# Two persistent two-bank PSUM tiles become a pool of tiles: two-bank for the first batch, then four single-bank tiles in rotation

## The chip, the cores and the metric

The kernel runs on one core of one Trainium2 chip. The metric is the device time of one execution in microseconds; the runs of a kernel are given by their median. The times of the stages come from one profiled execution.

The core's engines work from queues of their own, each in the order of the program, and wait for each other through semaphores: PE multiplies matrices into PSUM, ACT and DVE read PSUM and work element by element, POOL works on SBUF only, SP issues most of the DMAs (ACT and POOL issue some too). PSUM has 8 banks of 512 fp32 columns by 128 partitions; the kernel uses all of them.

## The reference

Attention at two scales for 8 batches of 8 heads, 576 positions of 64 values, followed by a two-layer network over all 4608 tokens:

```python
q_d = q.reshape(B, H, Sd, 4, D).mean(axis=3)      # k_d, v_d alike: Sd = 144 coarse positions
out_up = np.repeat(sm_attn(q_d, k_d, v_d), 4, axis=2)
mask = np.abs(pos[:, None] - pos[None, :]) < 4    # local attention
out_local = softmax(where(mask, scale * q @ k.T, -1e9)) @ v
x = (out_up + out_local).transpose(0, 2, 1, 3).reshape(4608, 512)
h = x @ w_in                                      # 512 -> 2048
g = np.where(h > 0.0, h, np.exp(np.minimum(h, 0.0)) - 1.0)
out = g @ w_out                                   # 2048 -> 512
```

## The kernel before

**Attention.** A batch is done in four pairs of heads. `pair_transposes` (L568) turns q and k of a pair around on PE into the PSUM tiles tq and tk, adds the coarse sums of v on PE into the free columns of tq, and has ACT copy them to qt and kt and DVE copy vd; POOL forms the coarse sums of q and k from the copies. `pair_scores` (L579) multiplies local and coarse scores into two PSUM tiles sc; ACT takes exp of each in two parts (pex, dex, L278 and L283), DVE masks (mex, L293). `denominators` (L307) sums the exps of all four pairs on PE into one bank den, and DVE takes the reciprocal rc (L333). `spread_out` and `spread_in` (L337, L341) send rc to DRAM and read it back spread over partitions (rd, rcb); ACT's queue issues these DMAs. `pair_outputs` (L602) multiplies exps and v for two pairs into two tiles lg, DVE multiplies by rcb (gn, ln, L427 and L430), and POOL adds both into xt (L438), the transposed input of the network. `first_batch` (L509) does batch 0 in a form of its own, on the two duo tiles and the tiles tagged "two".

**The network.** Tokens go in 9 blocks t of 512. `mm1(t, fc)` (L448) forms 128 of the 2048 hidden values of a block with four matmuls into one bank hp (L454). ACT reads the bank for e = exp (L459), DVE takes min and subtracts 1 (L460), and DVE reads the bank again for gt = max(hp, 0) + e (L463), which is the bank's last reader. `mm2(t, i)` (L467) does a quarter of the 16 matmuls of 128 tokens into a bank op (L474); with the last quarter ACT copies op to os (L480) and SP writes it out.

**PSUM.** Four of the 8 banks are two buffers of two banks each, tagged "two" (L96), which tq, tk, sc, lg and others take in turn. The other four are the tiles duo[0] and duo[1] (L99), two banks each, which live through the whole kernel. After the first batch, `bank(i)` (L297) gives bank i of these four: mm1 takes banks 0 and 1 (duo[0]) in turn, except in block 0, which takes 0, 2, 1, 3; `misc_bank` (L300) gives 2 and 3 (duo[1]) in turn to den and op.

**The order of the work** is written out by hand as a list of events with times (L609 to L645), sorted once. The unit is a slot: `mm1(t, s)` stands at 16t + s + 0.25 and `mm2(t, s)` at 16(t + 1) + s + 0.75, so that each slot from 16 to 143 holds one mm1 of block t and one mm2 of the block before; the last 16 slots hold mm2 alone. Batch b >= 3 starts at base = 16b - 25: its transposes stand at base + 0, 1.6, 4.8 and 9.7, its scores at base + 3.2, 6.4, 11.3 and 12.9, denominators at 14.5, `spread_out` and `spread_in` at 16.1 and 17.1, its outputs at 21 and 22.6, in the middle of the next batch. Batch 1 stands beside block 0, batch 2 from slot 12 on in a denser order. The last outputs are at slot 109.6, so slots 111 to 143 hold the network alone.

Of the kernel before, what the change touches and what calls it, by code (L numbers as in the profile page):

```python
# [10 lines left out]
FP32 = mybir.dt.float32  # L11
AB = mybir.AluOpType
AF = mybir.ActivationFunctionType
# [59 lines left out]
def kernel(  # L73
# [9 lines left out]
    nc = tc.nc  # L83
    sb = ctx.enter_context(tc.tile_pool(name="sb", bufs=1))
    ps = ctx.enter_context(tc.tile_pool(name="ps", bufs=1, space=bass.MemoryType.PSUM))
# [10 lines left out]
    def two(name):  # L96
        return ps.tile([128, 1024], FP32, tag="two", bufs=2, name=name)

    duo = [ps.tile([128, 1024], FP32, tag=f"duo{i}", bufs=1, name=f"duo{i}") for i in range(2)]  # L99

    def g2(ap, a, n):

# [2 lines left out]
    def h2(ap):  # L105
        return ap.rearrange("p (g u) -> p g u", g=2)
# [3 lines left out]
    WI = sb.tile([128, DMC, DFF], FP16, tag="WI", bufs=1, name="WI")  # L110
    WO = sb.tile([128, FCN, DM], FP16, tag="WO", bufs=1, name="WO")
# [134 lines left out]
    def scores(b, j, e, sc, masked):  # L246
        s = st[(b, j)]
        r = slice(64 * e, 64 * e + 64)
        if masked:
            for g in range(2):  # L250
                nc.tensor.matmul(
                    sc[0:KW, 512 * g : 512 * g + HB], C["NI"][:, 0:KW],
                    C["NI"][:, KW + HB * g : KW + HB * g + HB], start=True, stop=False,
                )
        for c in range(NB):
            a = 512 * (c // 3) + QB * (c % 3)
            nc.tensor.matmul(
                sc[0:KW, a : a + QB], s["kt"][r, QB * c : QB * c + KW],
                s["qt"][r, QB * c : QB * c + QB], start=not masked,
                stop=not masked or c % 3 == 2,  # L260
            )

    def coarse(b, j, e, sc):
        s = st[(b, j)]
        r = slice(64 * e, 64 * e + 64)
        for kg in range(2):
            nc.tensor.matmul(
                sc[0:KG, 512 * kg + HB : 512 * kg + HB + SD],
                s["kd"][r, KG * kg : KG * kg + KG], s["qd"][r, :], start=True, stop=True,
            )  # L270

    def exp_local(b, j, e, sc):
        s = st[(b, j)]
        if e == 0:
            s["pex"] = sb.tile([KW, 2, S], FP16, tag="mex" if b == 0 else "pex",
                               bufs=8 if b == 0 else 2, name="pex")
            s["dex"] = sb.tile([KG, 2, 2, SD], FP16, tag="dex", bufs=8, name="dex")
        nc.scalar.activation(  # L278
            out=h2(s["pex"][:, e, :]), in_=g2(sc[0:KW], 0, HB), func=AF.Exp, scale=SCALE
        )  # L280

    def exp_coarse(b, j, e, sc):
        nc.scalar.activation(  # L283
            out=st[(b, j)]["dex"][:, e], in_=g2(sc[0:KG], HB, SD), func=AF.Exp,
            scale=SCALE / 16,
        )
# [5 lines left out]
        mk2 = bass.AP(tensor=mk.tensor, offset=mk.offset, ap=[list(mk.ap[0]), [0, 2], [1, S]])  # L292
        nc.vector.tensor_tensor(out=s["mex"][:], in0=s["pex"][:], in1=mk2, op=AB.mult)  # L293

    misc = [0]

    def bank(i, n=512):  # L297
        return duo[i // 2][:, 512 * (i % 2) : 512 * (i % 2) + n]

    def misc_bank():  # L300
        misc[0] += 1
        return bank(2 + misc[0] % 2)


    RC = {}

    def denominators(b):  # L307
        den = misc_bank()
        for j in range(NPAIR):
            nc.tensor.matmul(  # L310
                den[32 * j : 32 * j + 32, 0:HB], C["SEED"][:, 32:64], C["SEED"][:, 64 + SD :],
                start=True, stop=False, tile_position=(0, 32 * j),
            )
        for e in range(2):
            for g in range(2):
                r = 2 * e + g
                for j in range(NPAIR):
                    nc.tensor.matmul(
                        den[32 * j : 32 * j + 32, 0:HB], C["IND"][0:KW, 31 - r : 63 - r],
                        st[(b, j)]["mex"][:, e, HB * g : HB * g + HB],  # L320
                        start=False, stop=False, tile_position=(0, 32 * j),
                    )
        for e in range(2):
            for kg in range(2):
                r = 4 + e
                for j in range(NPAIR):
                    nc.tensor.matmul(
                        den[32 * j : 32 * j + 32, 0:SD], C["IND"][0:KG, 31 - r : 63 - r],
                        st[(b, j)]["dex"][:, e, kg, :], start=False,
                        stop=(e == 1 and kg == 1), tile_position=(0, 32 * j),  # L330
                    )
        rc = RC[b] = sb.tile([128, HB], FP16, tag="rc", bufs=1, name="rc")
        nc.vector.reciprocal(out=rc[:], in_=den[:, 0:HB])  # L333
# [112 lines left out]
    gts, ops = {}, {}  # L446

    def mm1(t, fc):  # L448
        if fc == 0:
            gts[t] = sb.tile([128, FCN, TBLK], FP16, tag="gt", bufs=2, name="gt")  # L450
        hp = bank((0, 2, 1, 3)[fc % 4]) if t == 0 else bank(fc % 2)
        x = xts[t]
        for dc in range(DMC):
            nc.tensor.matmul(  # L454
                hp, WI[:, dc, 128 * fc : 128 * fc + 128], x[:, dc, :],
                start=(dc == 0), stop=(dc == DMC - 1),
            )
        e = sb.tile([128, TBLK], FP16, tag="e", bufs=3, name="e")
        nc.scalar.activation(out=e[:], in_=hp, func=AF.Exp)  # L459
        nc.vector.tensor_scalar(  # L460
            out=e[:], in0=e[:], scalar1=1.0, scalar2=-1.0, op0=AB.min, op1=AB.add
        )
        nc.vector.scalar_tensor_tensor(  # L463
            out=gts[t][:, fc, :], in0=hp, scalar=0.0, op0=AB.max, in1=e[:], op1=AB.add
        )

    def mm2(t, i):  # L467

        tt, part = i // 4, i % 4
        if part == 0:  # L470
            ops[t] = misc_bank()
        op_ = ops[t]
        for fc in range(4 * part, 4 * part + 4):
            nc.tensor.matmul(  # L474
                op_, gts[t][:, fc, 128 * tt : 128 * tt + 128], WO[:, fc, :],
                start=(fc == 0), stop=(fc == FCN - 1),
            )
        if part == 3:
            os_ = sb.tile([128, DM], FP32, tag="os", bufs=3, name="os")
            nc.scalar.copy(out=os_[:], in_=op_)  # L480
            r = TBLK * t + 128 * tt
            nc.sync.dma_start(out=out[r : r + 128, :], in_=os_[:])

# [25 lines left out]
    def first_batch():  # L509
        b = 0  # L510
        transposes(b, 0)
        evict_q(b, 0, act)
        evict_k(b, 0, act)
        sums(b, 0, "q")
        sums(b, 0, "k")
        load_qk(1, 0)
        for j in range(NPAIR):
            for e in range(2):
                scores(b, j, e, duo[e], True)
            if j < 3:  # L520
                transposes(b, j + 1)
            exp_local(b, j, 0, duo[0])
            exp_local(b, j, 1, duo[1])
            for e in range(2):
                coarse(b, j, e, duo[e])
            if j < 3:
                evict_q(b, j + 1, act)
            exp_coarse(b, j, 0, duo[0])
            if j < 3:
                evict_k(b, j + 1, act)  # L530
                sums(b, j + 1, "q")
                sums(b, j + 1, "k")
                load_qk(1, j + 1)
            exp_coarse(b, j, 1, duo[1])
            st[(b, j)]["mex"] = st[(b, j)]["pex"]
        for j in range(NPAIR):
            load_v(1, j)
        for h in range(2):
            dv = two("dv") if h == 0 else duo[0]
            den_half(b, h, dv)  # L540
            for i in range(2):
                v_sums(b, 2 * h + i, dv[0:KG, 512 + 256 * i : 768 + 256 * i], 128)
            vd = sb.tile([KG, 512], FP16, tag="vd2", bufs=2, name="vd2")
            dve(out=vd[:], in_=dv[0:KG, 512:1024])
            rbs = {}
            for i in range(2):
                j = 2 * h + i
                st[(b, j)]["vd"] = vd[:, 256 * i : 256 * i + 256]
                rbs[j] = two("rb")
                spread_pe(b, j, rbs[j])  # L550
            for i in range(2):
                j = 2 * h + i
                copy = act if h == 1 else dve
                spread_copy(b, j, rbs[j], copy, copy)
            for i in range(2):
                j = 2 * h + i
                lg = two("lg") if h == 0 else duo[i]
                outputs(b, j, lg)
                normalise(b, j, lg)
        for n in range(8):  # L560
            load_wo(n)
# [46 lines left out]

    at(-10, first)  # L609
    at(-9, first_batch)  # L610

    def loads(b, j):
# [62 lines left out]
```

## Time and profile before

| What | Value |
|---|---|
| median of 3 runs | 542.28 us (539.0 to 543.46) |
| profiled execution, its own time | 540.33 us |
| its span, first to last instruction | 538.5 us |
| mean granted TensorE clock | 0.971 |
| PE busy | 391.8 us (73%) |
| DVE busy | 233.5 us (43%) |
| ACT busy | 201.9 us (37%) |
| POOL busy | 143.3 us (27%) |
| mm1 matmuls (L454): busy, idle before them | 155.5 us, 92.3 us |
| mm2 matmuls (L474): busy, idle before them | 150.4 us, 16.5 us |

The first mm1 starts at 41.5 us, the first mm2 at 95.7, the mm1 of slot 39 at 178.7, that of slot 103 at 403.3, that of slot 111 at 427.1, and the mm2 of the last block alone begin at 518.3.

How to read the profile: a line of the waits names the engine and line that stood idle, what it waited for, the total in us, the number of times and the longest. A line of the timeline has start and duration in us, engine, line, operation, tile written <- tiles read, shape, xcount, and in brackets the idle time ahead of it and what ended it. PE's duration of a group runs to the end of its last matmul, so groups that follow without a gap overlap a little in the rows. A line of the windows has the stretch, its length, the busy time of PE, PEld (weight load), DVE, ACT and POOL with counts, the granted clock, the share of the DMA engines and GB/s.

### The profile page before, as it was taken

What the parts mean: (1) busy time and instruction counts of PE and PEld (TensorE: products, weight loads), DVE (VectorE), ACT (ScalarE), POOL (GpSimd) and SP (SyncE); (2) the same over time, 40 slices, a digit from 0 to 9 for tenths busy, and PEclk for the clock granted to TensorE, in tenths of its full rate; (3) what the DMA queues carried; (4) which work ended last, traced back from release to release, by engine and by line L of the source; (5) the groups of instructions that cost most, each with busy time, mean ns of one, the idle gap of its engine ahead of it and who ended that gap; (6) DMA issues with size and microseconds to landing.
All of it is one profiled execution on the core that took longest, in us unless ns stands there. A gap on an engine that the chain in (4) does not pass through costs nothing.

```text
span 538.5 us, 8199 instructions
## 1 busy us (share of the span) xinstructions
PE 391.8 (73%) x3164; PEld 208.0 (39%) x3164; DVE 233.5 (43%) x431; ACT 201.9 (37%) x377; POOL 143.3 (27%) x241
## 2 busy tenths in 40 slices
PE   4875966877886867776686778776766766676676
PEld 3663543443443444344344434343332322222232
DVE  2252765335455355524544464446443633333320
ACT  4601753453334344524362535253432222222211
POOL 4418444342340333213421252035200300000000
PEclk9999996899799999989999999899999999999999
DMA  9999998375540771348143934020002000000011
GB/s 188 209 195 172 201 177 158 71 154 129 116 90 21 164 145 48 63 114 161 39 107 75 176 60 110 7 74 21 21 25 75 27 34 19 19 21 39 19 40 58
DMA packets 130884, 49.02 MB, mean 91 GB/s; under 512 B 115324, under 2 KB 126238, under 8 KB 130846
## 3 DMA queue, kind: packets, MB, share of 16 engines
q1 hardware_dynamic: 115018, 36.97, 32.8%
q0 software_dynamic: 6480, 5.38, 6.3%
q10 hardware_dynamic: 9348, 6.16, 5.2%
q8 instruction: 25, 0.41, 0.3%
q14 instruction: 13, 0.11, 0.1%
HBM read 43.91 MB, written 9.95 MB: 100 GB/s over the span
## 4 chain that ended last, share of the span: by engine, by line
PE 45%; DVE 24%; ACT 17%; issue 5%; ACTq 3%; POOL 3%; DMA 3%; DVEq 0%; POOLq 0%
PE duo L454 21%; DVE gt L463 11%; PE duo L474 11%; ACT e L459 9%; DVE e L460 6%; ACTq L346 3%; ACT pex L278 3%; DVE rc L333 3%; PE tk L199 2%; ACT dex L283 2%; PE tq L199 2%; PE lg L411 2%; DMA rd<-rc 2%; DVE mex L293 2%; PE tq L240 1%
## 5 line engine op out<-in xcount | busy, mean ns | idle before, releaser
L454 PE MATMUL duo<-xt,WI 128*128 128x512 f16 x576 | 155.5, 392 | 92.3 <-DVE gt L463 86.6
L459 ACT ACTIVATE e<-duo 128x512 f16<-128x512 f32 x144 | 86.0, 599 | 241.9 <-PE duo L454 232.2
L474 PE MATMUL duo<-WO,gt 128*128 128x512 f16 x576 | 150.4, 388 | 16.5 <-DVE rc L333 13.7
L460 DVE TENSOR_SCALAR e<-e 128x512 f16<-128x512 f16 x144 | 48.0, 333 | 191.7 <-ACT e L459 191.1
L454 PEld LDWEIGHTS <-WI 128*128 128x128 f16 x576 | 54.9, 99 | 172.6 <-issue 115.9
L463 DVE SCALAR_TENSOR_TENSOR gt<-duo,e 128x512 f16<-128x512 f32 x144 | 99.6, 692 | 5.4
L474 PEld LDWEIGHTS <-gt 128*128 128x128 f16 x576 | 55.5, 99 | 84.4 <-issue 23.9
L232 POOL TENSOR_TENSOR t<-qt 128x288 f32<-128x288 f16 x28 | 18.6, 664 | 189.0 <-ACT qt L212 189.0
L438 POOL TENSOR_TENSOR xt<-ln,gn 128x512 f16<-128x512 f16 (+7 forms) x64 | 41.9, 685 | 82.8 <-DVE ln L430 82.8
L278 ACT ACTIVATE pex<-sc 112x576 f16<-112x576 f32 x56 | 36.2, 647 | 8.4 <-PE sc L593 7.6
L212 ACT CAST qt<-tq 128x576 f16<-128x576 f32 x32 | 20.4, 638 | 36.7 <-PE tq L240 32.6
L293 DVE TENSOR_TENSOR mex<-pex,MASK 112x1152 f16<-112x1152 f16 x28 | 21.9, 782 | 25.1 <-ACT pex L278 25.1
L480 ACT COPY os<-duo 128x512 f32<-128x512 f32 x36 | 21.1, 586 | 22.6 <-PE duo L474 22.6
L181 POOL CAST v<-v 112x768 f16<-112x768 f32 x32 | 27.2, 864 | 6.9 <-DMA v<-in_v_dram 6.7
L575 DVE CAST vd<-tq 72x256 f16<-72x256 f32 x28 | 11.7, 419 | 30.9 <-ACT qt L212 30.9
L411 PE MATMUL lg<-mex,v 112*64 112x96 f16 x336 | 14.1, 228 | 12.8 <-ACT dex L283 6.8
L283 ACT ACTIVATE dex<-sc 72x288 f16<-72x288 f32 x56 | 22.6, 404 | 0.0
L430 DVE TENSOR_TENSOR ln<-lg,rcb 128x576 f16<-128x576 f32 x30 | 22.4, 748 | 0.0
L199 PEld LDWEIGHTS tq<-I,q 96*128 96x128 f32 x168 | 18.4, 149 | 8.5 <-issue 2.8
L411 PEld LDWEIGHTS <-v 112*64 112x64 f16 x384 | 14.4, 129 | 17.9 <-issue 14.1
L218 ACT CAST kt<-tk 128x576 f16<-128x576 f32 x32 | 20.6, 644 | 0.1
L199 PE MATMUL tq<-I,q 96*128 96x96 f32 x168 | 19.7, 256 | 1.1 <-ACT dex L283 1.1
(74 smaller groups left out, 293.2 us busy)
## 6 DMA issues: line engine op xcount, KB each, us to landing
v<-in_v_dram SPq DMA_DIRECT2D x30, 336.0 KB, 4.9
out_dram<-os SPq DMA_DIRECT2D x36, 256.0 KB, 2.0
q<-in_q_dram SPq DMA_DIRECT2D x56, 144.0 KB, 3.3
k<-in_k_dram SPq DMA_DIRECT2D x56, 144.0 KB, 3.9
rcb<-rd ACTq DMA_DIRECT2D x14, 288.0 KB, 5.0
WO<-in_moe_w_out_dram POOLq DMA_DIRECT2D x8, 256.0 KB, 8.9
WI<-in_moe_w_in_dram POOLq DMA_DIRECT2D x3, 512.0 KB, 11.6
rcb<-rd ACTq DMA_DIRECT2D x14, 72.0 KB, 5.0
```

What stands on the lines that cost most here:

```text
L181: nc.gpsimd.tensor_copy(out=v16[:], in_=v32[:].rearrange("p (e c) d -> p c e d", e=2))
L199: nc.tensor.transpose(t[:, a : a + QB], x[:, c, :, :].rearrange("p e d -> p (e d)"), C["I32"][:])
L278: nc.scalar.activation(out=h2(s["pex"][:, e, :]), in_=g2(sc[0:KW], 0, HB), func=AF.Exp, scale=SCALE)
L283: nc.scalar.activation(out=st[(b, j)]["dex"][:, e], in_=g2(sc[0:KG], HB, SD), func=AF.Exp, scale=SCALE / 16,)
L293: nc.vector.tensor_tensor(out=s["mex"][:], in0=s["pex"][:], in1=mk2, op=AB.mult)
L411: nc.tensor.matmul(lg[64 * e : 64 * e + 64, a : a + QB], v16[:, c, e, :], s["mex"][:, e, QB * c : QB * c + QB], start=True, stop=True,)
L438: nc.gpsimd.tensor_tensor(out=xt(t)[:, j, t0 - TBLK * t : t1 - TBLK * t], in0=ln[:, a:z], in1=_rep4(gn[:, a // 4 : z // 4]), op=AB.add,)
L454: nc.tensor.matmul(hp, WI[:, dc, 128 * fc : 128 * fc + 128], x[:, dc, :], start=(dc == 0), stop=(dc == DMC - 1),)
L459: nc.scalar.activation(out=e[:], in_=hp, func=AF.Exp)
L460: nc.vector.tensor_scalar(out=e[:], in0=e[:], scalar1=1.0, scalar2=-1.0, op0=AB.min, op1=AB.add)
L463: nc.vector.scalar_tensor_tensor(out=gts[t][:, fc, :], in0=hp, scalar=0.0, op0=AB.max, in1=e[:], op1=AB.add)
L474: nc.tensor.matmul(op_, gts[t][:, fc, 128 * tt : 128 * tt + 128], WO[:, fc, :], start=(fc == 0), stop=(fc == FCN - 1),)
```

## The change

The two tiles duo[0] and duo[1] are no longer made once. For the first batch they come from a pool `fp` of their own, a new tile for every use (`duo(i, name)`). At the first call of `bank` that pool is closed and a pool `late` opened on the four banks, with two tags of two single-bank buffers each: "hp" for mm1, "misc" for den, op, and the odd fc of block 0. Every den, op and hp is now a tile of its own. Which buffer comes next is still taken in turn, and the events and the operations are the same.

```diff
-    duo = [ps.tile([128, 1024], FP32, tag=f"duo{i}", bufs=1, name=f"duo{i}") for i in range(2)]
+    front = ctx.enter_context(ExitStack())
+    fp = front.enter_context(tc.tile_pool(name="fp", bufs=1, space=bass.MemoryType.PSUM))
+    late = {}
+
+    def duo(i, name):
+        return fp.tile([128, 1024], FP32, tag=f"duo{i}", bufs=1, name=name)
...
-    misc = [0]
-
-    def bank(i, n=512):
-        return duo[i // 2][:, 512 * (i % 2) : 512 * (i % 2) + n]
-
-    def misc_bank():
-        misc[0] += 1
-        return bank(2 + misc[0] % 2)
-
+    def bank(tag, name):
+        if not late:
+            front.close()
+            late["ps"] = ctx.enter_context(
+                tc.tile_pool(name="late", bufs=1, space=bass.MemoryType.PSUM)
+            )
+        return late["ps"].tile([128, 512], FP32, tag=tag, bufs=2, name=name)
...
-        den = misc_bank()
+        den = bank("misc", "den")
...
-        hp = bank((0, 2, 1, 3)[fc % 4]) if t == 0 else bank(fc % 2)
+        hp = bank("misc" if t == 0 and fc % 2 else "hp", "hp")
...
-            ops[t] = misc_bank()
+            ops[t] = bank("misc", "op")
...
         for j in range(NPAIR):
+            sc = [duo(e, "sc") for e in range(2)]
             for e in range(2):
-                scores(b, j, e, duo[e], True)
+                scores(b, j, e, sc[e], True)
...
-            dv = two("dv") if h == 0 else duo[0]
+            dv = two("dv") if h == 0 else duo(0, "dv")
...
-                lg = two("lg") if h == 0 else duo[i]
+                lg = two("lg") if h == 0 else duo(i, "lg")
```

In first_batch the operands `duo[0]` and `duo[1]` of the exps and coarse scores become `sc[0]` and `sc[1]`; in mm1 and mm2 `hp` and `op_` become `hp[:]` and `op_[:]`.

More of the change, by code (lines that the diff above doesn't have):

```diff
@@ L454, in mm1 @@
             nc.tensor.matmul(
-                hp, WI[:, dc, 128 * fc : 128 * fc + 128], x[:, dc, :],
+                hp[:], WI[:, dc, 128 * fc : 128 * fc + 128], x[:, dc, :],
                 start=(dc == 0), stop=(dc == DMC - 1),
@@ L458, in mm1 @@
         e = sb.tile([128, TBLK], FP16, tag="e", bufs=3, name="e")
-        nc.scalar.activation(out=e[:], in_=hp, func=AF.Exp)
+        nc.scalar.activation(out=e[:], in_=hp[:], func=AF.Exp)
         nc.vector.tensor_scalar(
@@ L463, in mm1 @@
         nc.vector.scalar_tensor_tensor(
-            out=gts[t][:, fc, :], in0=hp, scalar=0.0, op0=AB.max, in1=e[:], op1=AB.add
+            out=gts[t][:, fc, :], in0=hp[:], scalar=0.0, op0=AB.max, in1=e[:], op1=AB.add
         )
@@ L474, in mm2 @@
             nc.tensor.matmul(
-                op_, gts[t][:, fc, 128 * tt : 128 * tt + 128], WO[:, fc, :],
+                op_[:], gts[t][:, fc, 128 * tt : 128 * tt + 128], WO[:, fc, :],
                 start=(fc == 0), stop=(fc == FCN - 1),
@@ L479, in mm2 @@
             os_ = sb.tile([128, DM], FP32, tag="os", bufs=3, name="os")
-            nc.scalar.copy(out=os_[:], in_=op_)
+            nc.scalar.copy(out=os_[:], in_=op_[:])
             r = TBLK * t + 128 * tt
@@ L517, in first_batch @@
         for j in range(NPAIR):
+            sc = [duo(e, "sc") for e in range(2)]
             for e in range(2):
-                scores(b, j, e, duo[e], True)
+                scores(b, j, e, sc[e], True)
             if j < 3:
                 transposes(b, j + 1)
-            exp_local(b, j, 0, duo[0])
-            exp_local(b, j, 1, duo[1])
+            exp_local(b, j, 0, sc[0])
+            exp_local(b, j, 1, sc[1])
             for e in range(2):
-                coarse(b, j, e, duo[e])
+                coarse(b, j, e, sc[e])
             if j < 3:
                 evict_q(b, j + 1, act)
-            exp_coarse(b, j, 0, duo[0])
+            exp_coarse(b, j, 0, sc[0])
             if j < 3:
@@ L533, in first_batch @@
                 load_qk(1, j + 1)
-            exp_coarse(b, j, 1, duo[1])
+            exp_coarse(b, j, 1, sc[1])
             st[(b, j)]["mex"] = st[(b, j)]["pex"]
```

## The prediction

> **What bounds the kernel now.** I read the share of busy time first (PE 73%, DVE 43%, ACT 37%: no engine is full), then the list of waits, and there who holds up PE, since PE has the most work.
>
> ```profile
> PE duo L454 <- DVE gt L463: 86.6, 96, 1.8
> PE duo L474 <- DVE rc L333: 13.7, 6, 2.5
> PE lg L411 <- ACT dex L283: 6.8, 9, 1.4
> PE lg L411 <- DVE vd L575: 4.9, 4, 1.2
> PE duo L474 <- ACT os L480: 2.9, 4, 0.7
> ```
>
> PE stands for 86.6 us in 96 waits ahead of mm1 (L454) until VectorE has written gt (L463), which is the last reader of an mm1 bank. Which group's gt? The timeline of the late stage, where only mm1 and mm2 are left, shows it:
>
> ```profile
> 454.83 1.02 PE L454 MATMUL duo<-xt,WI 128*128 128x512 f16 x4 [0.88 <-DVE gt L463]
> 455.69 1.03 PE L474 MATMUL duo<-WO,gt 128*128 128x512 f16 x4
> 455.90 0.60 ACT L459 ACTIVATE e<-duo 128x512 f16<-128x512 f32 x1 [2.17 <-PE duo L454]
> 456.53 0.29 DVE L460 TENSOR_SCALAR e<-e 128x512 f16<-128x512 f16 x1 [1.74 <-ACT e L459]
> 456.86 0.69 DVE L463 SCALAR_TENSOR_TENSOR gt<-duo,e 128x512 f16<-128x512 f32 x1
> 457.60 1.02 PE L454 MATMUL duo<-xt,WI 128*128 128x512 f16 x4 [0.88 <-DVE gt L463]
> ```
>
> The mm1 at 457.60 starts 0.05 after the gt that belongs to the mm1 of 454.83, its direct predecessor, although the two write different banks (fc % 2). So the two halves of one duo tile are held apart as if they were one buffer, and each slot is a serial chain matmul, exp, min, add, matmul of 2.77 us. PE's own part is 454.83 to 455.69 (0.86) and about as much for mm2. The same holds for duo1: mm2 waits for the reciprocal (rc) and for os, which read its other bank.
>
> Then the stages, by windows (us, PE, PEld, DVE, ACT, POOL, clock, DMA share, GB/s): slots 16 to 38, four periods of 16 slots with one batch of attention each, slots 103 to 110, and the 33 slots without attention.
>
> ```profile
> 96.00:178.60 82.60, 64.91 (x553) 35.36 (x552) 38.51 (x69) 35.38 (x68) 23.56 (x39) 0.92 0.43 95
> 178.60:236.00 57.40, 42.43 (x370) 22.66 (x368) 26.56 (x49) 23.28 (x44) 17.01 (x28) 0.97 0.48 99
> 291.60:348.40 56.80, 42.28 (x367) 22.66 (x365) 26.36 (x49) 23.28 (x44) 17.23 (x29) 0.97 0.48 100
> 403.30:427.10 23.80, 16.85 (x128) 7.64 (x128) 12.14 (x24) 5.95 (x10) 4.86 (x8) 1.00 0.19 54
> 427.10:518.20 91.10, 62.30 (x264) 25.51 (x264) 32.33 (x66) 24.92 (x42) 0.41 (x1) 1.00 0.06 24
> ```
>
> In a period of 57 us DVE works 26.5, ACT 23.3, POOL 17 and DMA 27 (0.48): a PE that goes faster has room on all of them down to about 40 us.
>
> **The change part by part.** *What it does not touch.* In the two compiled programs every engine has the same instructions in the same order (PE 5994, DVE 433, ACT 421, POOL 246, SP 184); no DMA is added or moved past another. Only PSUM addresses and waits differ. In the list of waits, an mm1 of t > 0 now waits for the gt two groups back, where it waited for one back; op and den wait for the reader two allocations back. So five prices, by stage.
>
> *1. The 33 last slots.* An mm1's gt is done 2.77 after its start (454.83 to 457.60). With two free banks the wait decides only if two slots are shorter than that. A slot of PE alone is 0.86 + 0.87 (326.76 to 327.62, 325.89 to 326.76) = 1.735, two are 3.47: no wait. DVE needs 0.33 + 0.69 and ACT 0.6 + 0.59/4 of it. 33 x 1.735 = 57.3 in place of 91.2: saves 33.9.
>
> *2. The last token block.* Its 64 mm2 run as 4 x 16 with 0.72 between for os; 16 take 3.61 with 0.16 of fill, 3.45 back to back. The stretch from 518.29 to 534.92 becomes 13.96: saves 2.7.
>
> *3. A period of 16 slots.* PE issue, from rows where the next one follows at once: 32 groups at 0.87 (27.8), 4 pairs' transposes at 1.33 (295.55 to 296.88), 4 scores at 0.57 (330.54 to 331.11), 2 output pairs at 0.89 (309.20 to 310.09), denominators 1.09 (125.55 to 126.64): 38.3. What stays: the tiles tagged "two" are not changed, and their waits remain.
>
> ```profile
> 309.20 0.45 PE L411 MATMUL lg<-mex,v 112*64 112x96 f16 x12 [1.24 <-DVE vd L575]
> 315.94 0.45 PE L411 MATMUL lg<-mex,v 112*64 112x96 f16 x12 [1.09 <-ACT dex L283]
> 316.78 0.45 PE L411 MATMUL lg<-mex,v 112*64 112x96 f16 x12 [0.26 <-ACT dex L283]
> 294.41 2.63 ACTq L346 DMA_DIRECT2D rcb<-rd  x4
> ```
>
> Outputs right behind transposes cost 1.24 to 1.4, right behind scores 1.35; both are set by ACT and DVE, not by duo. The third is new. ACT's queue issues four rcb transfers (2.63 us) once rd has landed, 2.4 after its issue (291.98 to 294.41). Today PE waits meanwhile anyway. Scheduled by hand from the period's first transposes: rd at 2.2, rcb issues 4.6 to 7.3, exp of the second slot to 7.9, second pair's kt copied by 9.1; PE reaches the scores that need this buffer at 7.9, so it waits 1.3. Sum 38.3 + 4.0 = 42.3. I carried the hand schedule through all 16 slots with the durations above: the nearest an mm1 comes to its gt is 0.76 (the slot behind the first scores, whose exps hold ACT for 1.77). The mm2 that waited 1.1 to 2.5 for rc goes straight on, since rc reads the other bank; DVE is held for the same 1.95, and the mm1 that needs the gt behind it stands two slots and a set of transposes later. Today's four periods last from 177.3 to 403.3, 226; 4 x 42.3 = 169: saves 57. Bounds: 38.3 with none of the stalls (16 more saved), and 47 if every one of the 8 transposes and scores adds 0.6 (19 less). I take 42.3, nearer to what the L411 rows show.
>
> *4. Slots 16 to 38* (95.7 to 177.3, 81.6). 23 x 1.74 + 6 transposes + 7 scores + 2 output pairs + 2 denominators = 40.0 + 8.0 + 4.0 + 1.8 + 2.2 = 56; the same kinds of stall (1.24, 1.35, 1.3 and some 0.9 for the xt of slot 32) 4.8; the slow start (mm2 at 95.70 takes 1.71, transposes 1.70) 1.2. 62: saves 20, bounds 12 and 24. *Slots 103 to 110*: 8 x 1.74 + 1.8 + 1.8 behind the last rcb issues = 17.5 in place of 23.8: saves 6.3.
>
> *5. Before 95.7: nothing.* In the first batch each tile is still taken when its forerunner's readers are done, as now. The pool's end makes the first mm1 wait for both last ln; its fourth matmul waits for xt (43.83) as before, so at most 0.7 and likely 0. The 2.82 that mm1 waits for rc at 76.3 goes, but the cover moves: ACT issues rcb from 81.13 to 83.75, so the transposes' copies and the scores at 84.99 come no sooner, and PE waits 5.4 there in place of 2.62. From 85 on outputs, ln and xt form the chain. 0, bounds 0 and 2.8.
>
> Sum: 33.9 + 2.7 + 57 + 20 + 6.3 = 119.9. The profiled span 538.5 becomes 418.6, and with the 1.83 around it (540.33 less 538.5) 420.4. The median of the runs (542.28) is 1.95 above that execution: 422.
>
> **A rule that speaks against it.** The granted clock is below 1 only around long gaps: 0.66 in 80 to 100, where PE stood 2.6 and 2.8 us; in the last stage, with a 0.88 gap in each slot, it is 1.00. The Trainium skill, "TensorE: Matmul & The Clock Gate", section "A second HAM failure mode: psum-queue depth-cycling", says that cycling through PSUM banks with N = 512 lets PE idle often enough for its clock to go up and down. Here, by the rows, gaps of 0.88 did not do that, so the trace does not bear it out; it is the third rival all the same.
>
> **The rivals.** *The waits come back elsewhere.* In-order ACT and DVE queues could keep mm1 waiting in slots 16 to 110, where exps (1.77), mask (0.76) and normalising (1.85) stand ahead of its own. Today 57.8 of the 86.6 lie there. If half survive, 29 and 5 of fills are lost: 456. For it: ACT e waits and DVE e waits are the largest rows after all. Against: ACT and DVE busy 23 and 26 in 42.
>
> *The change does nothing*: a new tile waits for all of the pool's readers, so the chain stands, 542. Against: the lists of waits name the gt two back.
>
> *The clock falls, and it gets slower.* PE issue from 95.7 on is 56 + 153 + 15.7 + 57 + 14 = 296 at full clock. If the denser bank cycling held the clock at c, 296 x (1/c - 1) is added; it eats the 119.9 at c = 0.71. At the 0.66 of 80 to 100 it is 152: 574. Only in the last 33 slots: 57.3 x 0.52 = 30, 452. Against: the matmul rows of 16 in a row (518.29, 3.61) ran at full clock.
>
> **How the numbers follow.** Forecast 0.82; waits elsewhere 0.11; clock in the last slots only 0.02; clock throughout 0.03; nothing 0.02. Faster by over 1% (about what a measurement of this kernel can tell from no change): 0.82 + 0.11 + 0.02 = 0.95; within 1% 0.02; slower 0.03. Range: down to 411 with about half of the period bound's 16 and a little of stage 4's, up to 442 with the 19 of the upper one; this leaves out the rivals.
>
> **What would show it.** The row "PE duo L454 <- DVE gt L463" nearly gone, late slots 1.74 apart, periods near 42, "PE L474 <- DVE rc" and "<- ACT os" gone, L411 waits as today or larger, PE about 92% of the span after 96, clock 1.00. Wrong: mm1 waits of a microsecond behind scores; slots of 2 us or more in the last stage; matmul rows above 0.4 us.

## The result, and the profile after

| | Before | After |
|---|---|---|
| median | 542.87 us (4 runs, 539.0 to 543.65) | 422.81 us (4 runs, 421.59 to 424.91) |
| profiled execution, span | 540.33 us, 538.5 us | 424.91 us, 423.1 us |
| PE busy, share of the span | 391.8 us, 73% | 371.9 us, 88% |

The ratio is 0.780 (95% interval 0.775 to 0.785). The forecast was 422 (411 to 442). Line numbers of the changed kernel are 3 to 5 higher: mm1 L457, exp L462, gt L466, mm2 L477, os L483, rcb L349.

First the waits of PE in the changed kernel. The row "PE duo L454 <- DVE gt L463" (86.6 us in 96 waits) has become the last of these, 1.9 us in 2 waits, and rows of mm2 on rc or os no longer exist. What stands on top now are users of the two-bank tiles tagged "two" (sc, lg), on ACT and DVE.

```profile
PE sc L590 <- DVE vd L579: 7.8, 4, 6.1
PE lg L414 <- ACT dex L288: 6.7, 10, 1.1
PE lg L414 <- DVE vd L579: 4.9, 4, 1.2
PE hp L457 <- DVE gt L466: 1.9, 2, 1.0
```

The timeline of the last stage shows how the chain came apart (start and duration first, in us):

```profile
348.56 1.03 PE L457 MATMUL hp<-xt,WI 128*128 128x512 f16 x4
349.42 1.03 PE L477 MATMUL op<-WO,gt 128*128 128x512 f16 x4
349.62 0.60 ACT L462 ACTIVATE e<-hp 128x512 f16<-128x512 f32 x1 [1.13 <-PE hp L457]
350.25 0.36 DVE L463 TENSOR_SCALAR e<-e 128x512 f16<-128x512 f16 x1 [0.24 <-ACT e L462]
350.28 1.03 PE L457 MATMUL hp<-xt,WI 128*128 128x512 f16 x4
350.64 0.69 DVE L466 SCALAR_TENSOR_TENSOR gt<-hp,e 128x512 f16<-128x512 f32 x1
```

The mm1 at 350.28 starts while the chain of its forerunner (348.56) has only come to the min; that forerunner's gt ends at 351.33. PE has no idle time in brackets, and a slot lasts 1.73 in place of 2.77, though exp and gt take as long as before (0.60 and 0.69). By windows (PE, PEld, DVE, ACT, POOL, clock, DMA share, GB/s) for the four periods, slots 103 to 110 and the 33 last slots:

```profile
159.60:204.00 44.40, 40.99 (x369) 22.73 (x367) 26.67 (x49) 23.18 (x44) 16.90 (x28) 0.96 0.62 127
204.00:248.40 44.40, 40.91 (x367) 22.62 (x365) 26.67 (x49) 23.18 (x44) 16.90 (x28) 0.96 0.65 128
248.40:291.10 42.70, 39.20 (x367) 22.20 (x365) 26.31 (x49) 23.18 (x44) 17.32 (x29) 1.00 0.68 133
291.10:331.50 40.40, 37.82 (x351) 20.68 (x349) 26.01 (x47) 23.17 (x44) 15.44 (x26) 1.00 0.15 47
331.50:348.50 17.00, 15.98 (x130) 7.66 (x128) 11.62 (x25) 5.85 (x11) 3.33 (x6) 1.00 0.31 80
348.50:405.50 57.00, 57.00 (x266) 25.83 (x264) 33.07 (x67) 24.38 (x41) 1.95 (x3) 1.00 0.10 38
```

ACT and DVE do the same work per period as before (23 and 26 to 27 us), in 43 us in place of 56; in the last line PE is busy all of the time. The first two lines have a granted clock of 0.96; that was not forecast, and is taken up below.

### The profile page after: what moved, and what is told of

The parts are those of the page before. It is cut to its first block, busy times and chain, and to the rows that moved or that the text cites. A ratio compares the mean times of both kernels' runs of the same rounds, so it can differ in the third digit from the quotient of the medians.

```text
span 423.1 us, 8180 instructions
## 1 busy us (share of the span) xinstructions
PE 371.9 (88%) x3164; PEld 205.9 (49%) x3164; DVE 234.0 (55%) x431; ACT 200.8 (47%) x377; POOL 143.1 (34%) x241
## 4 chain that ended last, share of the span: by engine, by line
PE 74%; ACT 6%; DVE 5%; POOL 4%; DMA 4%; ACTq 3%; issue 3%; DVEq 0%; POOLq 0%
PE op L477 28%; PE hp L457 26%; ACTq L349 3%; PE tk L204 3%; PE tq L204 3%; PE sc L590 2%; DMA rd<-rc 2%; POOL xt L441 2%; PE lg L414 2%; PE tq L245 2%; ACT e L462 2%; ACT dex L288 2%; ACT pex L283 1%; PE sc L262 1%; POOL WO L125 1%
## 5 line engine op out<-in xcount | busy, mean ns | idle before, releaser
L457 PE MATMUL hp<-xt,WI 128*128 128x512 f16 x576 | 154.2, 391 | 5.9 <-POOL xt L441 2.5
L462 ACT ACTIVATE e<-hp 128x512 f16<-128x512 f32 x144 | 86.0, 600 | 136.0 <-PE hp L457 114.8
L477 PE MATMUL op<-WO,gt 128*128 128x512 f16 x576 | 148.1, 385 | 0.0
L466 DVE SCALAR_TENSOR_TENSOR gt<-hp,e 128x512 f16<-128x512 f32 x144 | 99.6, 692 | 5.4
L463 DVE TENSOR_SCALAR e<-e 128x512 f16<-128x512 f16 x144 | 49.8, 346 | 86.3 <-ACT e L462 84.3
L457 PEld LDWEIGHTS <-WI 128*128 128x128 f16 x576 | 54.8, 100 | 70.4 <-issue 11.4
L477 PEld LDWEIGHTS <-gt 128*128 128x128 f16 x576 | 55.0, 99 | 66.0 <-issue 4.3
L283 ACT ACTIVATE pex<-sc 112x576 f16<-112x576 f32 x64 | 41.4, 648 | 11.7 <-PE sc L262 5.8
L483 ACT COPY os<-op 128x512 f32<-128x512 f32 x36 | 21.1, 586 | 18.8 <-PE op L477 18.8
L288 ACT ACTIVATE dex<-sc 72x288 f16<-72x288 f32 x64 | 25.9, 405 | 0.9 <-PE sc L272 0.9
L590 PE MATMUL sc<-qt,kt 64*112 64x96 f16 x336 | 15.5, 219 | 11.4 <-DVE vd L579 7.8
L414 PE MATMUL lg<-mex,v 112*64 112x96 f16 x336 | 12.2, 210 | 13.5 <-ACT dex L288 6.7
L590 PEld LDWEIGHTS <-kt 64*112 64x112 f16 x336 | 12.5, 129 | 22.9 <-issue 21.0
```

What stands on the lines that cost most here:

```text
L283: nc.scalar.activation(out=h2(s["pex"][:, e, :]), in_=g2(sc[0:KW], 0, HB), func=AF.Exp, scale=SCALE)
L288: nc.scalar.activation(out=st[(b, j)]["dex"][:, e], in_=g2(sc[0:KG], HB, SD), func=AF.Exp, scale=SCALE / 16,)
L414: nc.tensor.matmul(lg[64 * e : 64 * e + 64, a : a + QB], v16[:, c, e, :], s["mex"][:, e, QB * c : QB * c + QB], start=True, stop=True,)
L457: nc.tensor.matmul(hp[:], WI[:, dc, 128 * fc : 128 * fc + 128], x[:, dc, :], start=(dc == 0), stop=(dc == DMC - 1),)
L462: nc.scalar.activation(out=e[:], in_=hp[:], func=AF.Exp)
L463: nc.vector.tensor_scalar(out=e[:], in0=e[:], scalar1=1.0, scalar2=-1.0, op0=AB.min, op1=AB.add)
```

## The experiments

Two theories were set against each other. **By the tile**: before, a matmul into one half of a two-bank tile waits for readers of the other half, so two banks count as one buffer, and the change is worth what this wait costs. **From elsewhere**: two banks were enough as they were, and the gain comes from den and op, from the banks of block 0 or from the first batch's pool. What the changed kernel is bound by is a second question.

**hp as one tile again.** `bank("hp", ...)` hands out the halves of one persistent tile; all else is as changed.

```diff
+        if tag == "hp":
+            if "hp" not in late:
+                late["hp"] = late["ps"].tile([128, 1024], FP32, tag="hp", bufs=1, name="hp")
...
+            return late["hp"][:, 512 * (late["n"] % 2) : 512 * (late["n"] % 2) + 512]
```

> The changed kernel, but the two hp banks are the two halves of one persistent tile again; den and op stay single-bank tiles. Theory (a wait goes by the tile, so two banks in one tile count as one buffer): the wait of mm1 for the gt directly before it is back, slots of the last stage at 2.77 us, total 523 (518 to 530), that is the kernel before less what den and op gained (13.7 + 2.9 of waits and some slow restarts). Rival (the gain came from den, op, block 0 or the first batch's pool, and two banks of mm1 were enough as they were): about 423, slots at 1.73.

Measured: 519.41 (516.15 to 522.14), ratio to before 0.958 (0.952 to 0.963). Its own rows, the total of the waits and two late slots:

```profile
PE hp L463 <- DVE gt L472: 85.3, 99, 1.8
```

```profile
451.23 1.02 PE L463 MATMUL hp<-xt,WI 128*128 128x512 f16 x4 [0.88 <-DVE gt L472]
452.09 1.03 PE L483 MATMUL op<-WO,gt 128*128 128x512 f16 x4
454.00 1.02 PE L463 MATMUL hp<-xt,WI 128*128 128x512 f16 x4 [0.88 <-DVE gt L472]
```

The wait is back in full, 85.3 for 86.6, with 2.77 to a slot. The two banks are the same in number and are used in turn; only the tile is one.

**hp with a single bank.**

```diff
-        return late["ps"].tile([128, 512], FP32, tag=tag, bufs=2, name=name)
+        return late["ps"].tile([128, 512], FP32, tag=tag, bufs=1 if tag == "hp" else 2, name=name)
```

> The changed kernel with one single bank for hp in place of two (block 0 keeps misc for its odd groups). Theory: nothing is lost against two banks in one tile, within 1% of the run with hp as one tile (523), since the second bank there is never filled early. Rival: the second bank of one tile was worth something, and this is slower than that run by 2% or more.

Measured: 517.83 (515.01 to 522.25), ratio 0.956 (0.950 to 0.962), beside 0.958 of the run before.

```profile
PE hp L457 <- DVE gt L466: 85.2, 98, 1.7
```

85.2 us of waits with one bank, 85.3 with two in one tile: the second bank was worth nothing. The rival is out.

**den and op as one tile again**, hp split: as the first diff, with "misc" in place of "hp".

> The changed kernel, but den and op share the two halves of one persistent tile again; hp stays split. Theory: the waits of mm2 for rc (some 2.5 us, 6 of them, with up to 1 us of slow clock behind each) and for os in the last block (0.72, 4 times) are back, the last stage stays at 1.73 a slot: 445 (440 to 450). Rival (op's wait for rc was hidden behind something else, or mm2's op is also held in every slot): 423 to 426, or above 460.

Measured: 444.69 (442.24 to 445.75), ratio to before 0.820 (0.816 to 0.824).

```profile
PE misc L483 <- DVE rc L342: 13.7, 6, 2.5
PE misc L483 <- ACT os L489: 2.9, 4, 0.7
```

Both rows return with the very numbers of the kernel before, while the late slots stay at 1.73. So den and op bring about 22 of the 120 (444.69 less 422.81), hp about 97 (519.41 less 422.81); 119 together, and the two add up.

**The first batch's pool alone**: both late pairs are one tile each, the first batch as changed.

> The changed kernel with its pool for the first batch, but afterwards two persistent two-bank tiles again, one for hp and one for den and op. Theory (the first batch's pool is worth nothing by itself): as the kernel before, 543 (538 to 548), with its waits for gt, rc and os. Rival (part of the gain is from the first batch or from which banks are used): 535 or less.

Measured: 538.91 (536.13 to 545.23, 10 runs), ratio 0.997 (0.993 to 1.000): no more than a part in a hundred, if anything. With this the change is taken apart into all three parts.

**One more DVE operation in each mm1 group**, on both kernels. It lengthens only DVE's share of the chain, and changes no value.

```diff
+        nc.vector.tensor_scalar(
+            out=e[:], in0=e[:], scalar1=-1.0, scalar2=1.0, op0=AB.max, op1=AB.mult
+        )
```

On the kernel before:

> The kernel before with the same extra DVE operation of 0.33 us in every mm1 group (no value changes). Theory (the chain matmul, exp, min, add is what a slot lasts): the last stage goes from 2.77 to 3.10 a slot, 33 slots give 11, some 62 waits in the attention slots 20: 575 (568 to 582). Rival (DVE has idle time, 43% busy, so an added operation hides as in the changed kernel): 546 to 551.

On the changed kernel:

> The changed kernel with one more DVE operation of 0.33 us in every mm1 group, max(e, -1), which changes no value, between the min and gt. Theory (an mm1 now has two slots, 3.47 us, for a chain of 2.77): the chain becomes 3.1, the last stage stays at 1.73 a slot, and attention slots lose a few waits: 426 (423 to 431). Rival (DVE is the next bound, its in-order queue already late): 33 us or more on top, 456 and up.

Measured on the kernel before: 583.16 (580.98 to 586.48), ratio 1.075 (1.066 to 1.084), a little above the expected range. Its row of waits for gt grew by 31.8, from 86.6 to 118.4, where the expectation had counted 31 (11 and 20); what lies above the range is elsewhere in the kernel and was not taken apart.

```profile
PE duo L454 <- DVE gt L466: 118.4, 99, 2.0
```

Measured on the changed kernel: 430.59 (429.23 to 432.06), ratio to before 0.794 (0.790 to 0.799), where the changed kernel itself has 0.780. The late stage of the first and of the second:

```profile
550.19 1.02 PE L454 MATMUL duo<-xt,WI 128*128 128x512 f16 x4 [1.21 <-DVE gt L466]
552.21 0.29 DVE L463 TENSOR_SCALAR e<-e 128x512 f16<-128x512 f16 x1
552.54 0.69 DVE L466 SCALAR_TENSOR_TENSOR gt<-duo,e 128x512 f16<-128x512 f32 x1
553.28 1.02 PE L454 MATMUL duo<-xt,WI 128*128 128x512 f16 x4 [1.21 <-DVE gt L466]
```

```profile
380.12 1.03 PE L457 MATMUL hp<-xt,WI 128*128 128x512 f16 x4
380.42 0.29 DVE L466 TENSOR_SCALAR e<-e 128x512 f16<-128x512 f16 x1
380.74 0.69 DVE L469 SCALAR_TENSOR_TENSOR gt<-hp,e 128x512 f16<-128x512 f32 x1
381.85 1.03 PE L457 MATMUL hp<-xt,WI 128*128 128x512 f16 x4
```

In the kernel before, each slot grows from 2.77 to 3.09 by the operation that DVE, 43% busy, had plenty of time for; in the changed one the slot stays at 1.73. That is the difference between an engine's load and a chain's length. What it still costs the changed kernel lies almost all outside that stage. The two profiled executions differ by 5.7 (spans of 428.8 and 423.1): 3.7 before the first mm2 (99.8 in place of 96.1), 0.8 in slots 16 to 38, 0.6 in slots 103 to 110 and 0.9 from slot 111 on, of which 0.7 is one wait for gt in its second slot. The four periods together are 0.3 shorter: no matmul in them ran at half speed, which had cost the changed kernel 3.4 (last section).

**What is left: the rcb issues.** The rd and rcb transfers go from ACT's queue to SP's (`nc.scalar.dma_start` becomes `nc.sync.dma_start` in `spread_out` and `spread_in`).

> The changed kernel with the rd and rcb transfers issued from SP's queue in place of ACT's. Theory (the four rcb issues hold ACT's queue, and PE waits for kt behind them): the waits of scores for kt, 0.7 to 0.8 in three periods, and the 1.0 of slots 103 to 110 go, and of the 6.1 of stall at scores before 95 us a few; 418 (414 to 422). Rival (SP's in-order queue now holds the loads behind rc and rd, or the stall comes from DVE): 423 or more.

Measured: 417.32 (416.66 to 419.19), ratio to before 0.768 (0.763 to 0.774). The waits of scores for kt behind the rcb issues, which stand in the changed kernel's ACT queue like this, are gone from the periods, and the 1.0 of slots 103 to 110 too. Not all of the gain need be the queue's: in the profiled execution one stretch of matmuls runs at half speed, where the changed kernel's has two of 1.7 us each (last section).

```profile
207.01 2.67 ACTq L349 DMA_DIRECT2D rcb<-rd  x4
209.73 0.60 ACT L462 ACTIVATE e<-hp 128x512 f16<-128x512 f32 x1 [3.24 <-issue]
210.23 0.63 ACT L217 CAST qt<-tq 128x576 f16<-128x576 f32 x1
210.74 0.66 ACT L223 CAST kt<-tk 128x576 f16<-128x576 f32 x1
```

Before 95 us it went another way: scores came at 81.1 in place of 85.3, and PE then stood 5.9 behind ln, where it had stood 6.1 behind vd. The chain that ends last runs there through rc, rd, rcb, ln and xt, and the first mm2 starts at 95.7 in place of 96.1.

**What is left: the two-bank tiles.** Their users in batches 3 to 7 are spaced evenly:

```diff
-            base = 16 * b - 25
-            tr, sc_ = (0, 1.6, 4.8, 9.7), (3.2, 6.4, 11.3, 12.9)
-            d0, s0, s1, o0 = 14.5, 16.1, 17.1, (21, 22.6)
+            base = 16 * b - 26
+            tr, sc_ = (0, 1.6, 4.8, 11.2), (3.2, 9.6, 12.8, 14.4)
+            d0, s0, s1, o0 = 15.9, 17.3, 18.3, (22.4, 24)
```

> The changed kernel with other event times for batches 3 to 7, so that users of the two-bank tiles stand 1.6 slots apart throughout (base one slot earlier; transposes 0, 1.6, 4.8, 11.2; scores 3.2, 9.6, 12.8, 14.4; denominators 15.9, spreads 17.3 and 18.3, outputs 22.4 and 24). Theory (what is left in a period are the waits of the two-bank tiles, 1.24 and 1.35, and a stretch of matmuls at half clock behind them in two periods, 1.7): periods come to 40 or less, clock 1.00 there, total 409 (405 to 416). Rival (the waits only move to other users, or the later rcb holds up normalising and xt): 420 or more. If the half-clock stretch has to do with something else than these waits, it stays, at 412 to 414.

Measured: 414.72 (412.54 to 415.9), ratio to before 0.762 (0.757 to 0.768). The periods did what the theory said: 40.0, 39.7, 39.7 and less, and the clock in them is 1.00. That the clock is higher because these waits are gone is not shown: the changed kernel with the extra DVE operation has all of the waits, and its four periods read 1.00 too.

```profile
157.80:197.80 40.00, 39.51 (x368) 21.87 (x366) 28.16 (x50) 23.14 (x45) 17.12 (x28) 1.00 0.68 141
197.80:237.50 39.70, 39.10 (x365) 21.56 (x364) 27.48 (x49) 22.44 (x45) 17.13 (x28) 1.00 0.67 143
```

But from 131 to 134 us PE stood 2.97 for a gt, a new stall with slow matmuls behind it. ACT's rows ahead of it point to the cause: its four rcb issues took 5.28, and qt, kt and the exps stood behind them.

```profile
125.75 5.28 ACTq L349 DMA_DIRECT2D rcb<-rd  x4
131.13 0.64 ACT L217 CAST qt<-tq 128x576 f16<-128x576 f32 x1 [5.17 <-DMA rcb<-rd]
133.94 1.86 PE L457 MATMUL hp<-xt,WI 128*128 128x512 f16 x4 [2.97 <-DVE gt L466]
```

**Both together.**

> The respaced event times and the rd and rcb transfers on SP's queue together. Theory (the respaced kernel's wait of mm1 for gt, 2.97 at 133.9 and 0.5 to 0.6 in four later places, comes from the rcb issues on ACT's queue, and the slow matmuls behind the first of them from that wait): these go, 408 (404 to 412). Rival (the waits come from the normalising on DVE, or SP's queue holds loads too long at the closer spacing): 413 to 416, as the respaced kernel alone, or more.

Measured: 404.08 (402.0 to 405.1, 6 runs), ratio to before 0.746 (0.743 to 0.750), the fastest version. In its list of waits no mm1 waits for gt, so the stall did come from the rcb issues on ACT's queue; PE is busy 92% of a span of 400.2.

## Why the prediction was right

It named the step that decides (an mm1 waits for the gt one back because both banks are one tile), and the experiments bear that out: the wait returns with the tile (85.3) and is the same with one bank (85.2). By its terms, from the two profiled executions (the last block begins one mm2 after the row at 404.67):

| Term | Forecast | Measured |
|---|---|---|
| before the first mm2 | 0 | -0.4 (95.7 to 96.1) |
| slots 16 to 38 | 20 | 19.4 |
| four periods | 57 | 52.7 |
| slots 103 to 110 | 6.3 | 6.8 |
| 33 last slots | 33.9 | 34.2 |
| last block | 2.7 | 2.6 |
| sum | 119.9 | 115.4 |

- *The stalls that stay.* 1.24, 1.09 and 0.26 were read from the L411 rows of before and stand in every period after, to the hundredth. The new one behind the rcb issues was worked out as 1.3 and measured 0.72, 0.80 and 0.81; in the last period it is absent. Its mechanism is shown by the run with rcb on SP.
- *The term that was mis-sized is the period*: 43.3 on average from its transposes on, where 42.3 was said. In two of the four a stretch of matmuls runs at half speed (below), 1.7 each. And PE's issue is longer than the sum of groups: an mm1 ahead of scores or denominators takes 0.96 to the next start (221.10 to 222.06), not 0.87. The lower wait makes up part of it.
- *Before 95.7 nothing*: the first mm1 starts 0.8 later (42.34 for 41.51), as the pool's end was said to do up to 0.7, and the mm1 that had waited 2.82 for rc goes at 76.05; the scores behind it then wait 6.1 in place of 2.6, as the moved cover said (5.4).
- *Signs of being wrong.* Two that it named came up in small. An mm1 waited for gt by 1.02 (337.94), but behind the rcb issues of slots 103 to 110, where the forecast had put 1.8, and not behind scores. And matmuls took more than 0.4 in two periods (1.88 for four).
- *The rivals.* That ACT and DVE keep mm1 waiting: 1.9 us in 2 waits are left of 86.6, so no. That the clock falls with the denser use of the banks: in the 57 us in which two banks alternate without a gap it was 1.00, so not for that reason. Where matmuls ran at half speed, gaps stood ahead of them in both kernels, though often the same gaps had no such effect (last section). The section of the Trainium skill named in the prediction ("TensorE: Matmul & The Clock Gate", "A second HAM failure mode: psum-queue depth-cycling") is thus not borne out for cycling as such; its account of idling is the nearer one.
- *The clock before.* The prediction said that the clock is below 1 only around long gaps, of 2.6 and 2.8 us. That does not hold even for the kernel before: behind gaps of 1.18 and 1.39 outputs, mm2 and mm1 ran at half speed there from 142.91 on. The sum took full speed throughout the periods, so no term of it held the 3.4 that such stretches cost there.

```profile
142.91 0.69 PE L411 MATMUL lg<-mex,v 112*64 112x96 f16 x12 [1.39 <-ACT dex L283]
144.60 1.89 PE L474 MATMUL duo<-WO,gt 128*128 128x512 f16 x4
```

- *The median.* The sum gave 420.4 for the profiled execution, which took 424.91; the median was set 1.95 above it and lies 2.1 below. The sum was 4.5 short of the execution that it describes; that the median came within 1 of the forecast is luck.

## What to carry to other kernels

Look at which instance of the releaser ends a wait: when a matmul group waits for the reader of the group directly before it, though banks alternate, check whether the dependence is drawn around the tile. If it is, a tile for each bank is worth as much as the banks that were thought to be there. Price such a change by what a slot falls to: from the chain's length to the bound engine's own slot (2.77 to 1.73 here), if the chain fits into the slots that the buffers give it (2.77 against 2 x 1.73). Then look for the waits that the old one had covered, in the in-order queues above all: here DMA issues on ACT. Space the users of the remaining shared buffers by the time that each holds them.

## What the runs showed of the hardware that was not expected

Half-speed matmuls came behind a cluster of gaps none of which is longer than 1.24 us: 1.24, 1.09 and 0.26 within 7 us. The changed kernel, second period:

```profile
223.78 0.45 PE L414 MATMUL lg<-mex,v 112*64 112x96 f16 x12 [1.09 <-ACT dex L288]
224.61 0.45 PE L414 MATMUL lg<-mex,v 112*64 112x96 f16 x12 [0.26 <-ACT dex L288]
225.12 1.88 PE L477 MATMUL op<-WO,gt 128*128 128x512 f16 x4
226.79 1.91 PE L457 MATMUL hp<-xt,WI 128*128 128x512 f16 x4
228.50 1.07 PE L477 MATMUL op<-WO,gt 128*128 128x512 f16 x4
```

Two groups take 3.4 us where they would take 1.7, then the speed is back; the clock of that period reads 0.96. The gaps of 1.24 and 1.09 stand in each of the four periods of eight kernels here. Half speed came right behind them in the first and second period of the changed kernel, in the third alone with rcb on SP, in three periods with hp as one tile and in two with a single hp bank. It came behind them in no period of the kernel before, of the first batch's pool alone, of den and op as one tile, or of the changed kernel with the extra DVE operation, where the clock of all four periods reads 1.00. So these gaps alone do not bring it on. In the periods of the respaced kernel, which have none of these gaps, it did not come, but with the extra operation it did not come either, so that does not show that the gaps are needed. What decides between one period and the next stays open.

The same four rcb issues held ACT's queue for 2.58 us in the changed kernel, at 127.55, and for 5.28 in the respaced one, at 125.75. From 115 to 135 the DMA engines were busy 0.79 of the time in the first and 0.91 in the second; whether that is the reason was not tried.
